# The opening of a two-layer mixer kernel: V projection by rows of Wv, with the first two tiles centred instead of normalised

## The chip, the cores and the metric

The kernel runs on 1 core of one Trainium2 chip. The metric is the device time of one execution in microseconds (us), and lower is better. The profile counts from its own zero and gives a *span*, about 1.9 us shorter than the device time of the same run. Each timed run also leaves its span, and I use spans where tenths of a microsecond matter.

## The reference, cut to what matters

Two layers, each an attention block and a token-mixing MLP with residuals, on 2048 tokens of width 1024. Only the first step of the first block is touched: a layer norm of the input rows, then the projection with the V third of `wqkv`.

```python
def _A_ref(x, wqkv, wo):
    B, S, D = x.shape                      # 1, 2048, 1024
    qkv = (x @ wqkv).reshape(B, S, 3, H, Dh) ...
    q, k, v = qkv[0], qkv[1], qkv[2]
    ...                                    # local dilated attention, 32 heads
x = A_x                                    # bf16
x = x + _A_ref(_layernorm(x, axis=-1), A_wqkv, A_wo)
...                                        # MLP, then both again
```

## The kernel before

The tokens are 16 tiles of 128 rows. At the start each tile is loaded (`x_load`), its statistics are taken on VectorE (`S_` twice, then `A_`), its reciprocal deviation on ScalarE (`R_`: a logarithm, then an exponential), it is normalised on VectorE (`N_`), and it is transposed into `hT`. For tiles 0 to 4 the transposition is done by TensorE (`tr`) and copied by ScalarE (`C_`) out of PSUM, the memory that its results go to; for the others by the DMA (`T_`). Then V of tile k is 16 matmuls of 128x512 (`V_`: two column halves n, eight contraction rows kt), evacuated by ScalarE (`E_`). Each engine has one list of steps that it follows in order:

```python
def w_load(n, hf):     # a block of Wv: half the contraction rows of half the columns, 512 KB
    return nc.sync.dma_start(out=wv[n][hf][:], in_=wq_v[:, hf*(KD//2):(hf+1)*(KD//2), 2*D + n*512:2*D + (n+1)*512])
def R_(k):  rss[k] = st("rs", [P, 1]); return rsqrt(rss[k][:], mvs[k][:, 1:2], 1.0, eps1)
def tr(k):
    tps[k] = pss.tile([P, KD, P], BF16, name="s", tag="s")
    ...                                                    # 8 transposes of xs[k]
def E_(k, n):
    return nc.scalar.copy(out=v[c][i][:, n*512:(n+1)*512], in_=pss_[k, n][:])
... # 14 warm-up matmuls on zeros
... # loads: x0 in halves, x1, Wv(0,0), x2, Wv(0,1), x3, Wv(1,0), Wv(1,1), x4 ... x15
pe  = [(tr, 0), (V_, 0, 0, lo4), (tr, 1), (V_, 0, 0, hi4), (V_, 1, 0, lo4), (tr, 2), (V_, 1, 0, hi4),
       (V_, 2, 0, a8), (V_, 0, 1, a8), (tr, 3), (V_, 1, 1, a8), (V_, 2, 1, a8), (tr, 4)]
pe += [(V_, k, n, a8) for k in range(3, NT) for n in range(NDC)]
act = [(R_, 0), (C_, 0, 0), (R_, 1), (C_, 0, 1), (C_, 1, 0), (C_, 1, 1), (R_, 2), (E_, 0, 0), ...]
dve = [(S_, 0, 0), (S_, 0, 1), (A_, 0), (S_, 1, 0), (N_, 0, halves), (S_, 1, 1), (A_, 1), (N_, 1, whole), ...]
```

The softmax here doesn't subtract the row's maximum and nothing guards it: scores larger than these inputs give would overflow.

## Time and profile before

| | before |
|---|---|
| device time, median of 6 runs | 1293.74 us |
| span of the profiled run | 1291.8 us |
| first transposition / first V matmul | 6.52 / 7.80 us |
| first q/k matmul, where the V projection has ended | 65.79 us |

The page of the kernel before: the span, the busy times of the engines, and the chain of work that ended last, by engine and by line.

```profile
span 1291.8 us, 19417 instructions
...
PE 1275.1 (99%) x8286; PEld 593.4 (46%) x8442; DVE 417.1 (32%) x852; ACT 372.8 (29%) x628; POOL 2.4 (0%) x15
...
PE 98%; issue 1%; DVE 0%; ACT 0%
PE m L352 17%; PE s L594 15%; PE s L547 15%; PE m L467 8%; PE acc L547 7%; PE m L547 7%; PE acc L594 7%; PE m L594 7%; PE m L337 4%; PE m L255 4%; PE s L383 2%; PE acc L418 1%; PE acc L422 1%; PE m L268 0%; PE s L244 0%
```

TensorE (PE) is busy for 99% of the span and makes up 98% of the chain. A change outside TensorE can therefore win only where TensorE stands still or has nothing useful to do, and that is in the first twelve microseconds. (Later there are 31 pauses of about 0.16 us, 4.9 us in all, which wait for nothing that the profile shows.) Here is the chain in order of time (start, duration, what), from the first warm-up matmul:

```profile
1.38 5.30 PE m L268 x14
6.68 0.46 PE s L244 x8
...
7.16 0.59 ACT hT L249
...
7.80 1.04 PE m L255 x4
8.84 0.61 PE s L244 x8
...
9.47 1.07 ACT hT L249 x2
10.55 0.20 ACT ln L174
...
10.77 0.21 ACT rs L175
...
11.01 0.56 DVE x L188
...
11.61 0.62 PE s L244 x8
...
12.28 4.26 PE m L255 x19
```

Read it as a relay: each row was released by the one above it. TensorE transposes tile 0 until 7.14; the transposed rows are copied (ACT, 7.16); four V matmuls and tile 1's transposes follow; then the chain leaves TensorE for the copy, rsqrt and normalisation that tile 2's transposes need (9.47 to 11.6). After 12.28 it is TensorE alone. A row of another engine is not always idle time of TensorE, which had V matmuls to do for part of it. What it really waited in the first 90 us is in the waits (total, times, longest):

```profile
PE m L268 <- DVE warm L207: 1.4, 1, 1.4
PE m L255 <- ACT hT L249: 0.7, 1, 0.7
PE s L244 <- DVE x L188: 0.3, 1, 0.3
```

That is 1.0 us after the first transposition (the warm-up's 1.4 us is the start of the program), and the rest of what can be won is a sooner start. The V projection ends where this piece of the chain begins:

```profile
65.79 6.91 PE m L352 x32
```

From here on both kernels do the same work, so I use the start of this piece as a landmark: 1291.8 less 65.79 leaves 1226.0 us.

Why the first transposition comes only at 6.5 is in the timeline (start, duration, engine, line, operation, shapes):

```profile
3.22 1.29 DVE L226 BATCH_NORM_STATS2 bn<-x 128x6 f32<-128x512 bf16 x2 [1.89 <-DMA x<-in_A_x_dram]
...
4.54 0.21 DVE L230 BATCH_NORM_AGGREGATE mv<-bn 128x2 f32<-128x12 f32 x1
...
4.78 0.29 ACT L174 ACTIVATE ln<-mv,eps 128x1 f32<-128x1 f32 x1 [2.70 <-DVE mv L230]
5.11 0.20 ACT L175 ACTIVATE rs<-ln 128x1 f32<-128x1 f32 x1
...
5.34 0.69 DVE L226 BATCH_NORM_STATS2 bn<-x 128x6 f32<-128x512 bf16 x1 [0.59 <-DMA x<-in_A_x_dram]
...
5.95 0.72 DVE L188 TENSOR_SCALAR x<-x,mv,rs 128x512 bf16<-128x512 bf16 x2
```

Statistics of tile 0 end at 4.75. The rsqrt takes until 5.31. By then VectorE, which works in order, starts the statistics of tile 1, which have landed, and normalises tile 0 only at 5.95.

### The profile page before, as it was taken

What the parts mean: (1) busy time and instruction counts of PE and PEld (TensorE: products, weight loads), DVE (VectorE), ACT (ScalarE), POOL (GpSimd) and SP (SyncE); (2) the same over time, 40 slices, a digit from 0 to 9 for tenths busy, and PEclk for the clock granted to TensorE, in tenths of its full rate; (3) what the DMA queues carried; (4) which work ended last, traced back from release to release, by engine and by line L of the source; (5) the groups of instructions that cost most, each with busy time, mean ns of one, the idle gap of its engine ahead of it and who ended that gap; (6) DMA issues with size and microseconds to landing.
All of it is one profiled execution on the core that took longest, in us unless ns stands there. A gap on an engine that the chain in (4) does not pass through costs nothing.

```text
span 1291.8 us, 19417 instructions
## 1 busy us (share of the span) xinstructions
PE 1275.1 (99%) x8286; PEld 593.4 (46%) x8442; DVE 417.1 (32%) x852; ACT 372.8 (29%) x628; POOL 2.4 (0%) x15
## 2 busy tenths in 40 slices
PE   9999999999999999999999999999999999999999
PEld 4444444444444444444444444444444444444444
DVE  7457777820000022322300667778100000111111
ACT  5456664431111110000023666644311111000000
POOL 0000000000000000000000000000000000000000
PEclk9999999999999999999999999999999999999999
DMA  8411123742222235466410111247423222334330
GB/s 236 82 46 47 51 82 120 212 139 82 65 82 76 57 110 139 131 154 142 130 33 1 47 50 51 79 151 214 120 65 89 75 60 81 103 106 136 117 92 33
DMA packets 201862, 125.54 MB, mean 97 GB/s; under 512 B 39984, under 2 KB 183600, under 8 KB 201776
## 3 DMA queue, kind: packets, MB, share of 16 engines
q1 hardware_dynamic: 201776, 124.30, 34.2%
q8 instruction: 66, 1.08, 0.4%
q14 instruction: 20, 0.16, 0.0%
HBM read 96.48 MB, written 16.78 MB: 88 GB/s over the span
## 4 chain that ended last, share of the span: by engine, by line
PE 98%; issue 1%; DVE 0%; ACT 0%
PE m L352 17%; PE s L594 15%; PE s L547 15%; PE m L467 8%; PE acc L547 7%; PE m L547 7%; PE acc L594 7%; PE m L594 7%; PE m L337 4%; PE m L255 4%; PE s L383 2%; PE acc L418 1%; PE acc L422 1%; PE m L268 0%; PE s L244 0%
## 5 line engine op out<-in xcount | busy, mean ns | idle before, releaser
L594 PEld LDWEIGHTS <-w 128*128 128x128 bf16 x1820 | 177.0, 98 | 210.2
L547 PEld LDWEIGHTS <-w 128*128 128x128 bf16 x1792 | 175.3, 98 | 211.4
L352 PE MATMUL m<-hT,wqk 128*128 128x512 bf16 x963 | 223.3, 379 | 6.2 <-issue 4.6
L547 PE MATMUL s<-h,w 128*128 128x512 bf16 x878 | 201.2, 379 | 0.8
L594 PE MATMUL s<-g,w 128*128 128x512 bf16 (+1 forms) x912 | 201.0, 374 | 0.7
L596 DVE SCALAR_TENSOR_TENSOR xo<-s,b_sb,xs 128x512 bf16<-128x512 f32 (+1 forms) x33 | 24.4, 739 | 532.9 <-PE s L594 530.8
L352 PEld LDWEIGHTS <-wqk 128*128 128x128 bf16 x1024 | 95.3, 98 | 117.9 <-issue 10.7
L398 DVE TENSOR_TENSOR Pm<-pc,band 32x640 bf16<-32x640 bf16 x256 | 123.5, 483 | 56.3 <-ACT pc L386 49.4
L467 PE MATMUL m<-wo,oT 128*128 128x512 bf16 x500 | 110.6, 379 | 0.8 <-issue 0.3
L547 PE MATMUL acc<-h,w 128*128 128x512 bf16 x440 | 103.1, 379 | 0.5
L594 PE MATMUL acc<-g,w 128*128 128x512 bf16 x436 | 99.7, 379 | 0.5
L547 PE MATMUL m<-h,w 128*128 128x512 bf16 x438 | 98.5, 379 | 0.5
L594 PE MATMUL m<-g,w 128*128 128x512 bf16 (+1 forms) x436 | 96.9, 376 | 0.6
L174 ACT ACTIVATE ln<-mv,eps 128x1 f32<-128x1 f32 x64 | 18.9, 295 | 221.1 <-DVE mv L182 184.9
L467 PEld LDWEIGHTS <-oT 128*128 128x128 bf16 x512 | 49.6, 98 | 60.3 <-issue 1.3
L554 ACT ACTIVATE g<-s,b_sb 128x1024 bf16<-128x1024 f32 x28 | 31.2, 1114 | 158.2 <-PE s L547 146.4
L363 DVE COPY qB<-qs 32x512 bf16<-32x512 bf16 x136 | 38.1, 280 | 99.2 <-ACT qs L359 97.1
L255 PE MATMUL m<-wv,hT 128*128 128x512 bf16 x250 | 55.6, 379 | 1.0 <-ACT hT L249 0.7
L337 PE MATMUL m<-wv,hT 128*128 128x512 bf16 x251 | 55.2, 379 | 0.3
L386 ACT ACTIVATE pc<-s,shift 128x640 bf16<-128x640 f32 x64 | 51.2, 800 | 11.7 <-PE s L383 11.7
L359 ACT CAST qs<-m 128x512 bf16<-128x512 f32 x64 | 37.5, 586 | 48.7 <-PE m L352 47.6
L356 ACT CAST kT<-m 128x512 bf16<-128x512 f32 x64 | 37.5, 586 | 46.4 <-PE m L352 46.4
(58 smaller groups left out, 671.8 us busy)
## 6 DMA issues: line engine op xcount, KB each, us to landing
w<-in_B_w_dram SPq DMA_DIRECT2D x56, 512.0 KB, 3.8
w<-in_B_w_dram SPq DMA_DIRECT2D x64, 448.0 KB, 4.7
wqk<-in_A_wqkv_dram SPq DMA_DIRECT2D x16, 512.0 KB, 5.2
xa<-xn SPq DMA_DIRECT2D x32, 256.0 KB, 2.3
xs<-xa SPq DMA_DIRECT2D x32, 256.0 KB, 3.0
wv<-in_A_wqkv_dram SPq DMA_DIRECT2D x8, 512.0 KB, 5.6
wo<-in_A_wo_dram SPq DMA_DIRECT2D x8, 512.0 KB, 6.4
xr<-in_A_x_dram SPq DMA_DIRECT2D x16, 256.0 KB, 3.4
```

The costliest lines, as they stand in the source:

```text
L255: r = nc.tensor.matmul(pss_[k, n][:], lhsT=hT[:, kt, cols(*order[k])], rhs=wv[n][kt // 4][:, kt % 4, :], start=(kt == 0), stop=(kt == KD - 1))
L337: nc.tensor.matmul(ps[:], lhsT=hT[:, kt, cols(c, i)], rhs=wv[n][kt // 4][:, kt % 4, :], start=(kt == 0), stop=(kt == KD - 1))
L352: mm = nc.tensor.matmul(ps[:], lhsT=wts[part][:, kt, (g % 2) * P:(g % 2 + 1) * P], rhs=hT[:, kt, lo:lo + 512], start=(kt == 0), stop=(kt = ...
L356: nc.scalar.copy(out=kT[u % 2][:, ls], in_=ps[:])
L359: nc.scalar.copy(out=qs[:], in_=ps[:])
L363: nc.vector.tensor_copy(out=qB[u % 2][hp, h, ls], in_=qs[hp, :])
L386: nc.scalar.activation(out=pc[:].rearrange("p (n t) h k -> p n (t h k)", n=2), in_=ss[:, :, 0:2 * HG * GW], func=ACT.Exp, scale=scale, bia ...
L398: mm = nc.vector.tensor_tensor(out=Pm[rp, :, s0:s0 + HB, r * KG:r * KG + GW].rearrange("p h t k -> p t h k"), in0=pc[rp], in1=mk, op=ALU.mult)
L467: mm = nc.tensor.matmul(ps[:], lhsT=oT[g][:, cols(c, i)], rhs=wo[n][g // 4][:, g % 4, :], start=(g == 0), stop=(g == NG - 1))
L547: nc.tensor.matmul(pairs[fl][0][dc], lhsT=wt[c][:, i, fl * P:(fl + 1) * P], rhs=h2[c][i][:, dc * 512:(dc + 1) * 512], start=(k == 0), stop ...
L554: nc.scalar.activation(out=g[fb][:, fl, :].rearrange("p (n d) -> p n d", n=2), in_=t[:], func=ACT.Gelu_apprx_tanh, bias=b1_sb[:, ft:ft + 1])
L594: nc.tensor.matmul(ap, lhsT=w2t[ft // HF][:, ft % HF, c::DIL], rhs=g[ft // GF][:, ft % GF, lo:lo + w], start=(ft == 0), stop=(ft == FT - 1))
```

## The change: its intent and the diff

The intent is to have TensorE at work sooner and without gaps.

- Layer norm is (x - mean) times one number per row, and that number can be applied after the projection. Tiles 0 and 1 are only centred before their transposes, half of tile 0 on each of VectorE and ScalarE, and the evacuation of V multiplies by the reciprocal deviation. No rsqrt stands before the first matmul.
- The q and k projections need the normalised rows in `hT`. So tiles 0 and 1 are normalised later and written over the centred ones by two more DMA transposes, in the middle of those of the other tiles.
- Wv is loaded by contraction rows (256 KB, all columns) in place of four blocks of 512 KB. TensorE goes through tiles 0 and 1 row by row, four matmuls to a row.
- A tile of V collects in one PSUM tile of two banks and is evacuated at once; two rsqrt steps follow each evacuation.
- Warm-up matmuls: nine, and one more after tile 0's transposes, in place of 14.

```diff
-        def w_load(n, hf):
-            return nc.sync.dma_start(out=wv[n][hf][:], in_=wq_v[:, hf * (KD // 2):(hf + 1) * (KD // 2), ...])
+        def w_load(kt):
+            return nc.sync.dma_start(out=wv[kt // 2][:, kt % 2, :], in_=wq_v[:, kt, 2 * D:3 * D])
...
+        def B_(k):      # minus the mean, for ScalarE
+            return nc.vector.tensor_scalar(out=nm0[:], in0=mvs[k][:, 0:1], scalar1=-1.0, scalar2=None, op0=ALU.mult)
+        def M_(k, h):
+            return nc.vector.tensor_scalar(out=xc[k][:, h], in0=xs[k][:, h], scalar1=mvs[k][:, 0:1], scalar2=None, op0=ALU.subtract)
+        def Ma(k, h):
+            return nc.scalar.activation(out=xc[k][:, h], in_=xs[k][:, h], func=ACT.Identity, bias=nm0[:])
...                     # E_ takes a whole tile
-            return nc.scalar.copy(out=v[c][i][:, n * 512:(n + 1) * 512], in_=pss_[k, n][:])
+            if k < 2:
+                return nc.scalar.activation(out=dst, in_=src, func=ACT.Identity, scale=rss[k])
+            return nc.scalar.copy(out=dst, in_=src)           # 128x1024
...                     # loads in the new order; nine warm-ups; the old lists
+        pe = [(tr, 0), (W_, 1), *VV(0, 0), (tr, 1), *VV(0, 1, 2), *VV(1, 0, 1, 2)]
+        for kt in range(3, 6):
+            pe += [*VV(0, kt), *VV(1, kt)]
+        pe += [(tr, 2), *VV(0, 6, 7), *VV(1, 6, 7), (V_, 2, 0, a8), (tr, 3), (V_, 2, 1, a8), (tr, 4)]
+        act = [(Ma, 0, halves[1]), (C_, 0, 0), (C_, 0, 1), (C_, 1, 0), (C_, 1, 1), (R_, 0), (R_, 1), (R_, 2), (C_, 2, 0), (C_, 2, 1),
+               (R_, 3), (E_, 0), (E_, 1), (R_, 4), ...]
...                     # VectorE: tile 0 is centred before tile 1's statistics
+            if k in (8, 9):
+                dve.append((N_, k - 8, whole))
+        sp = [(T_, k) for k in (*range(np_, 10), 0, 1, *range(10, NT))] + [(load_biases,)]
...                     # layer two's Wv in the same layout
```

More of the change, by code (lines that the diff above doesn't have):

```diff
@@ L113, in ln_exp_table @@
         return tc.keep_in_program_order(nc.scalar.preload_act_table_set("natural_log_exp_and_others"))
-    ln_exp_table()
     ident = const.tile([P, P], BF16, name="ident")
@@ L133 @@
                                 pattern=[[-1, GW]], channel_multiplier=1)
+    mv01 = const.tile([P, 2, 2], FP32, name="mv01")
+    rs01 = const.tile([P, 2], FP32, name="rs01")
+    nm0 = const.tile([P, 1], FP32, name="nm0")
     b1_bf = const.tile([P, FT], BF16, name="b1_bf")
@@ L187, in norm_dve @@
     def norm_dve(dst, x, mean, rs):
-        return nc.vector.tensor_scalar(out=dst, in0=x, scalar1=mean, scalar2=rs[:], op0=ALU.subtract, op1=ALU.mult)
+        return nc.vector.tensor_scalar(out=dst, in0=x, scalar1=mean, scalar2=rs, op0=ALU.subtract, op1=ALU.mult)
     def norm_act(dst, x, mean, rs):
@@ L205, in start_up @@
         np_ = 5
+        xc = [x2(f"xc{k}") for k in range(2)]
         warm = x2("warm", [P, 512])
@@ L217, in x_load @@
             return r
-        def w_load(n, hf):
-            return nc.sync.dma_start(out=wv[n][hf][:], in_=wq_v[:, hf * (KD // 2):(hf + 1) * (KD // 2),
-                                                                2 * D + n * 512:2 * D + (n + 1) * 512])
+        def w_load(kt):
+            return nc.sync.dma_start(out=wv[kt // 2][:, kt % 2, :], in_=wq_v[:, kt, 2 * D:3 * D])
         def S_(k, cc):
@@ L228, in A_ @@
         def A_(k):
-            mvs[k] = st("mv", [P, 2])
-            return nc.vector.bn_aggr(out=mvs[k][:], in_=sts[k][:])
+            mvs[k] = mv01[:, k, :] if k < 2 else st("mv", [P, 2])[:]
+            return nc.vector.bn_aggr(out=mvs[k], in_=sts[k][:])
+        def B_(k):
+            return nc.vector.tensor_scalar(out=nm0[:], in0=mvs[k][:, 0:1], scalar1=-1.0, scalar2=None, op0=ALU.mult)
+        def M_(k, h):
+            return nc.vector.tensor_scalar(out=xc[k][:, h], in0=xs[k][:, h], scalar1=mvs[k][:, 0:1], scalar2=None,
+                                           op0=ALU.subtract)
+        def Ma(k, h):
+            return nc.scalar.activation(out=xc[k][:, h], in_=xs[k][:, h], func=ACT.Identity, bias=nm0[:])
         def R_(k):
-            rss[k] = st("rs", [P, 1])
-            return rsqrt(rss[k][:], mvs[k][:, 1:2], 1.0, eps1)
+            rss[k] = rs01[:, k:k + 1] if k < 2 else st("rs", [P, 1])[:]
+            return rsqrt(rss[k], mvs[k][:, 1:2], 1.0, eps1)
         def N_(k, hs):
@@ L241, in tr @@
         def tr(k):
-            tps[k] = pss.tile([P, KD, P], BF16, name="s", tag="s")
+            tps[k] = psm.tile([P, KD, P], BF16, name="m", tag="m")
             for kt in range(KD):
-                r = nc.tensor.transpose(tps[k][:, kt, :], xs[k][:, kt * P:(kt + 1) * P], ident[:])
+                r = nc.tensor.transpose(tps[k][:, kt, :], (xc[k] if k < 2 else xs[k])[:, kt * P:(kt + 1) * P], ident[:])
             return r
@@ L251, in V_, with E_ @@
         def V_(k, n, kts):
-            if kts[0] == 0:
-                pss_[k, n] = m_tile()
+            if k not in pss_:
+                pss_[k] = a_tile() if k % 3 == 1 else s_tile()
             for kt in kts:
-                r = nc.tensor.matmul(pss_[k, n][:], lhsT=hT[:, kt, cols(*order[k])], rhs=wv[n][kt // 4][:, kt % 4, :],
+                r = nc.tensor.matmul(pss_[k][:, n, :], lhsT=hT[:, kt, cols(*order[k])], rhs=wv[kt // 2][:, kt % 2, n * 512:(n + 1) * 512],
                                      start=(kt == 0), stop=(kt == KD - 1))
             return r
-        def E_(k, n):
+        def E_(k):
             c, i = order[k]
-            return nc.scalar.copy(out=v[c][i][:, n * 512:(n + 1) * 512], in_=pss_[k, n][:])
+            dst, src = v[c][i][:].rearrange("p (n d) -> p n d", n=NDC), pss_[k][:]
+            if k < 2:
+                return nc.scalar.activation(out=dst, in_=src, func=ACT.Identity, scale=rss[k])
+            return nc.scalar.copy(out=dst, in_=src)
         def T_(k):
@@ L266, in start_up, with W_ @@
         wm = m_tile()
-        for _ in range(14):
-            chain_("PE", lambda: nc.tensor.matmul(wm[:], lhsT=warm[:, 0:P], rhs=warm[:], start=True, stop=True))
+        def W_(n):
+            for _ in range(n):
+                r = nc.tensor.matmul(wm[:], lhsT=warm[:, 0:P], rhs=warm[:], start=True, stop=True)
+            return r
+        for _ in range(9):
+            chain_("PE", W_, 1)
         halves = (slice(0, D // 2), slice(D // 2, D))
         whole = (slice(0, D),)
+        chain_("ACT", ln_exp_table)
@@ L272, in start_up @@
         chain_("SP", x_load, 0, halves)
         chain_("SP", x_load, 1)
-        chain_("SP", w_load, 0, 0)
+        for kt in range(4):
+            chain_("SP", w_load, kt)
         chain_("SP", x_load, 2)
-        chain_("SP", w_load, 0, 1)
+        chain_("SP", w_load, 4)
+        chain_("SP", w_load, 5)
         chain_("SP", x_load, 3)
-        chain_("SP", w_load, 1, 0)
-        chain_("SP", w_load, 1, 1)
+        chain_("SP", w_load, 6)
+        chain_("SP", w_load, 7)
         for k in range(4, NT):
@@ L281, in start_up, with VV @@
             chain_("SP", x_load, k)
-        lo4, hi4 = range(KD // 2), range(KD // 2, KD)
+        def VV(k, *kts):
+            return [(V_, k, n, [kt]) for kt in kts for n in range(NDC)]
         a8 = range(KD)
-        pe = [(tr, 0), (V_, 0, 0, lo4), (tr, 1), (V_, 0, 0, hi4), (V_, 1, 0, lo4), (tr, 2), (V_, 1, 0, hi4),
-              (V_, 2, 0, a8), (V_, 0, 1, a8), (tr, 3), (V_, 1, 1, a8), (V_, 2, 1, a8), (tr, 4)]
+        pe = [(tr, 0), (W_, 1), *VV(0, 0), (tr, 1), *VV(0, 1, 2), *VV(1, 0, 1, 2)]
@@ L287, in start_up @@
+        for kt in range(3, 6):
+            pe += [*VV(0, kt), *VV(1, kt)]
+        pe += [(tr, 2), *VV(0, 6, 7), *VV(1, 6, 7), (V_, 2, 0, a8), (tr, 3), (V_, 2, 1, a8), (tr, 4)]
         pe += [(V_, k, n, a8) for k in range(3, NT) for n in range(NDC)]
-        act = [(R_, 0), (C_, 0, 0), (R_, 1), (C_, 0, 1), (C_, 1, 0), (C_, 1, 1), (R_, 2), (E_, 0, 0), (C_, 2, 0), (C_, 2, 1),
-               (E_, 1, 0), (R_, 3), (E_, 2, 0), (R_, 4), (E_, 0, 1), (C_, 3, 0), (C_, 3, 1), (R_, 5), (E_, 1, 1), (R_, 6),
-               (E_, 2, 1), (C_, 4, 0), (C_, 4, 1)]
@@ L291, in start_up @@
-        es = [(E_, k, n) for k in range(3, NT) for n in range(NDC)]
+        act = [(Ma, 0, halves[1]), (C_, 0, 0), (C_, 0, 1), (C_, 1, 0), (C_, 1, 1), (R_, 0), (R_, 1), (R_, 2), (C_, 2, 0), (C_, 2, 1),
+               (R_, 3), (E_, 0), (E_, 1), (R_, 4), (C_, 3, 0), (C_, 3, 1), (E_, 2), (C_, 4, 0), (C_, 4, 1), (R_, 5), (E_, 3), (R_, 6)]
         rs = [(R_, k) for k in range(7, NT)]
-        for j, e in enumerate(es):
-            act.append(e)
-            if rs and j % 4 != 3:
-                act.append(rs.pop(0))
@@ L297, in start_up @@
-        dve = [(S_, 0, 0), (S_, 0, 1), (A_, 0), (S_, 1, 0), (N_, 0, halves), (S_, 1, 1), (A_, 1), (N_, 1, whole),
+        for k in range(4, NT):
+            act.append((E_, k))
+            act += rs[:2]
+            del rs[:2]
+        dve = [(S_, 0, 0), (S_, 0, 1), (A_, 0), (B_, 0), (M_, 0, halves[0]), (S_, 1, 0), (S_, 1, 1), (A_, 1), (M_, 1, whole[0]),
                (S_, 2, 0), (S_, 2, 1), (A_, 2)]
@@ L300, in start_up @@
             nx = k + 1 < NT
-            if nx:
-                dve.append((S_, k + 1, 0))
-            dve.append((N_, k, whole))
+            if k == 2:
+                dve += [(N_, k, whole), (S_, k + 1, 0)]
+            else:
+                if nx:
+                    dve.append((S_, k + 1, 0))
+                dve.append((N_, k, whole))
             if nx:
                 dve += [(S_, k + 1, 1), (A_, k + 1)]
+            if k in (8, 9):
+                dve.append((N_, k - 8, whole))
         dve.append((zero_fill,))
         dve.append((cast_biases,))
-        sp = [(T_, k) for k in range(np_, NT)] + [(load_biases,)]
+        sp = [(T_, k) for k in (*range(np_, 10), 0, 1, *range(10, NT))] + [(load_biases,)]
         qs = {"PE": pe, "ACT": act, "DVE": dve, "SP": sp}
-        need = {cast_biases: lambda: (load_biases,) in done, R_: lambda k: k in mvs, N_: lambda k, h: k in rss, tr: lambda k: (N_, k) in done, C_: lambda k, hf: k in tps,
-                V_: lambda k, n, kts: ((C_, k, 1 if kts[-1] == KD - 1 else 0) in done or (T_, k) in done), E_: lambda k, n: (V_, k, n) in done,
-                T_: lambda k: (N_, k) in done}
+        need = {cast_biases: lambda: (load_biases,) in done, R_: lambda k: k in mvs, N_: lambda k, h: k in rss, tr: lambda k: (N_, k) in done if k > 1 else (M_, k) in done and (k == 1 or (Ma, k) in done),
+                B_: lambda k: k in mvs, M_: lambda k, h: k in mvs, Ma: lambda k, h: (B_, k) in done, C_: lambda k, hf: k in tps,
+                V_: lambda k, n, kts: ((C_, k, kts[-1] * 2 // KD) in done or (T_, k) in done), E_: lambda k: (V_, k, 1) in done and (k > 1 or k in rss),
+                T_: lambda k: (N_, k) in done and (k > 1 or (E_, k) in done)}
         done = set()
@@ L325, in load_wv, with fill_wv @@
     def load_wv():
-        return [[wt_("wv", [P, KD // 2, 512]) for _ in range(2)] for _ in range(NDC)]
-    def fill_wv(wv, n):
-        for hf in range(2):
-            nc.sync.dma_start(out=wv[n][hf][:],
-                              in_=wq_v[:, hf * (KD // 2):(hf + 1) * (KD // 2), 2 * D + n * 512:2 * D + (n + 1) * 512])
+        return [wt_("wv", [P, 2, D]) for _ in range(KD // 2)]
+    def fill_wv(wv):
+        for j in range(KD // 2):
+            nc.sync.dma_start(out=wv[j][:], in_=wq_v[:, 2 * j:2 * j + 2, 2 * D:3 * D])
     def v_proj(v, c, i, wv, ns):
@@ L336, in v_proj @@
             for kt in range(KD):
-                nc.tensor.matmul(ps[:], lhsT=hT[:, kt, cols(c, i)], rhs=wv[n][kt // 4][:, kt % 4, :],
+                nc.tensor.matmul(ps[:], lhsT=hT[:, kt, cols(c, i)], rhs=wv[kt // 2][:, kt % 2, n * 512:(n + 1) * 512],
                                  start=(kt == 0), stop=(kt == KD - 1))
@@ L603, in gemm2 @@
             mean, rs = stats(xo, 1.0, eps1)
-            norm_dve(xs[:], xo[:], mean, rs)
+            norm_dve(xs[:], xo[:], mean, rs[:])
             nc.sync.dma_start_transpose(out=hT[:, :, cols(c, i)], in_=xs[:])
@@ L619 @@
         else:
-            fill_wv(wv, 0)
-            fill_wv(wv, 1)
+            fill_wv(wv)
             wts = [None, None]
```

## The prediction

> **What bounds the kernel now.** The tensor engine: the page gives PE 1275.1 of 1291.8 us busy (99%), the chain that ended last is 98% PE. The change touches the opening (V projection of layer one, until the first q/k matmul at 65.79 us in the chain) and the layout of layer two's Wv, which the chain shows as unbroken PE work.
>
> **What it loses.** Timeline and chain: x0's first half reaches VectorE at 3.22, statistics end at 4.75, rsqrt on ScalarE 4.78 to 5.31, normalising 5.95 to 6.67 (held up by tile 1's statistics), transposes done 7.13, hT copy 0.59, first V matmul at 7.80. From there to 65.79 are 57.99 us. A V matmul costs 0.2159 us (208 in 44.9 us, from 20.9 on), 256 cost 55.3, four further transposes 4 x 0.5 = 2.0: about 0.7 us is lost after 7.80 (waits for the hT copy and for rsqrt and normalising of tile 2).
>
> **What changes.**
> - Tile 0 is centred, not normalised: a 128x1 step, then half on VectorE (0.36) and half on ScalarE (0.59) side by side. No wait for rsqrt (0.53) or tile 1's statistics. First transposes done near 6.0 instead of 7.13, first V matmul near 6.7.
> - Tile 1 landed at 5.34; its two statistics, aggregate and centring (1.3 + 0.21 + 0.55) let its transposes start near 7.5 instead of 8.81.
> - From there PE has work by rows of Wv (4 matmuls, 0.86 us, per 256 KB). By bytes moved in the DMA windows plus about 1.2 us to landing (fits x1 at 5.3, x4 at 13.7), rows 1, 2, 3 land near 7.1, 7.9, 8.8 and rows 6, 7 near 12.4, 13.2; PE wants them at 8.0, 8.5, 10.2, 13.3, 14.1.
> - Evacuations: one of 1024 (estimate 1.1 us from 1.114 us of the 1024 gelu) instead of two of 0.59. Rsqrt two per 3.45 us instead of three per 6.9.
> - Two normalisations (0.55 each) and two DMA transposes (median 3.1 us to landing) more; off the path.
> - Tightest wait: evacuation of tile 2 (near 20.2), tile 4's copies (21.3), rsqrt 5, normalising (22.4), DMA transpose 3.1: 25.6, against V of tile 5 at 26.3.
> - Layer two: Wv is loaded in the same four pieces from 601 us, needed at 649.6: nothing.
> - Warm matmuls 14 become 9 plus 1. The Trainium skill ("TensorE: Matmul & The Clock Gate", "What's actually happening") says full clock comes after about 3.4 us of activity in a free-running window; the trace agrees roughly: weight loads 0.43 us apart from 1.38 to 5.62, then 0.2. Nine end near 5.2, so the clock should still rise near 5.6.
>
> **Sum.** Tile 1's transposes end at 8.0; 254 matmuls 54.8, three transposes 1.5: V ends at 64.35 instead of 65.79. Gain 1.4 us: 1292.3 us, range 1291.6 to 1293.3. Faster by over 2%: 0; within 2%: 1.0; slower: 0.
>
> **What would show it.** First transposes near 5.4 to 6.0, first V matmul 6.7, tile 1's transposes at 7.5, first q/k matmul near 64.4, and every later distance unchanged (from first q/k matmul to the end 1226 us). No PE wait on Wv loads over 0.3 us in the waits.
>
> **What would make it wrong.** The clock rising one window later: V matmuls at 0.43 until about 9, costing 1 to 1.5 us, most of the gain. Rows of Wv landing over 1 us later than worked out. Tile 5's DMA transpose late (the slowest took 4.2 us to landing): up to 0.4 us.

## The result, and the profile after

| | before | after |
|---|---|---|
| device time, median of 6 runs | 1293.74 us | 1292.18 us |
| lowest to highest | 1293.43 to 1294.32 | 1292.02 to 1292.80 |
| span of the profiled run | 1291.8 us | 1290.6 us |
| first transposition / first V matmul | 6.52 / 7.80 us | 5.24 / 6.81 us |
| first q/k matmul (landmark) | 65.79 us | 64.48 us |

The medians differ by 1.56 us, and no run of one kernel reaches into the range of the other. The ratio is 0.9988 with a 95% interval of 0.9976 to 1.0001; a ratio is the mean time of one kernel's fast runs over that of the other's of the same rounds, so it is not quite the ratio of the medians. The page after:

```profile
span 1290.6 us, 19407 instructions
...
PE 1273.7 (99%) x8282; PEld 592.7 (46%) x8438; DVE 417.5 (32%) x854; ACT 370.9 (29%) x613; POOL 2.4 (0%) x15
...
PE 98%; issue 1%; DMA 0%; DVE 0%; SPq 0%
```

The chain of the changed kernel in order of time, to be held against the one of before:

```profile
1.72 3.85 DMA x<-in_A_x_dram
...
5.59 1.30 DVE bn L228 x2
...
6.92 0.22 DVE mv L232
...
7.16 0.50 DVE xc L238
...
7.70 0.62 PE m L256 x8
8.32 0.86 PE s L267 x4
...
64.48 6.91 PE m L383 x32
```

There is one relay left ahead of TensorE: the load of tile 1, its two statistics, aggregate and centring. Then it is TensorE alone, from 7.70 to the end of the V projection at 64.48. The copy out of PSUM, the rsqrt and the normalisation that stood between pieces of TensorE work before are gone from the chain. The start of the timeline shows how tile 0 got ahead:

```profile
4.84 0.34 DVE L238 TENSOR_SCALAR xc<-x,mv 128x512 bf16<-128x512 bf16 x1
4.96 0.72 ACT L242 ACTIVATE xc<-x,nm 128x512 bf16<-128x512 bf16 x1 [2.88 <-DVE nm L235]
...
5.24 0.89 PE L256 MATMUL m<-ident,xc 128*128 128x128 bf16 x8 [0.18 <-DVE xc L238]
...
6.81 0.60 PE L267 MATMUL s<-wv,hT 128*128 128x512 bf16 x2 [0.46 <-ACT hT L261]
```

The aggregate ends at 4.74. VectorE and ScalarE centre a half each, and the first four transposes run at 5.24 while ScalarE is still busy. What TensorE waited for in the first 90 us (total, times, longest):

```profile
PE m L256 <- DVE xc L238: 0.5, 2, 0.3
PE s L267 <- ACT hT L261: 0.5, 1, 0.5
```

Against the kernel before, the waits are no shorter in total (1.0 us in both), but they lie earlier: what is left is over at 7.70, where the kernel before still waits at 11.6, and the first V matmul runs 1.0 us sooner. Wv does not appear. The span less the landmark is 1226.1 us, as before (1226.0): the whole gain lies ahead of it.

### The profile page after: what moved, and what is told of

It is laid out like the page before. It is cut to its first block, busy times and chain, and to the rows that moved or that the text cites. A ratio compares the mean times of both kernels' runs of the same rounds, so it can differ in the third digit from the quotient of the medians.

```text
span 1290.6 us, 19407 instructions
## 1 busy us (share of the span) xinstructions
PE 1273.7 (99%) x8282; PEld 592.7 (46%) x8438; DVE 417.5 (32%) x854; ACT 370.9 (29%) x613; POOL 2.4 (0%) x15
## 4 chain that ended last, share of the span: by engine, by line
PE 98%; issue 1%; DMA 0%; DVE 0%; SPq 0%
PE m L383 17%; PE s L625 15%; PE s L578 15%; PE m L498 9%; PE acc L578 7%; PE m L578 7%; PE acc L625 7%; PE m L625 7%; PE m L368 4%; PE s L267 3%; PE s L414 2%; PE acc L267 1%; PE acc L449 1%; PE acc L453 1%; DMA x<-in_A_x_dram 0%
## 5 line engine op out<-in xcount | busy, mean ns | idle before, releaser
L368 PE MATMUL m<-wv,hT 128*128 128x512 bf16 x251 | 55.2, 379 | 0.3
L505 DVE TENSOR_TENSOR xn<-m,xr 128x512 bf16<-128x512 f32 x64 | 44.2, 690 | 16.9 <-PE m L498 16.4
```

The lines of the kernel that those rows point to most:

```text
L368: nc.tensor.matmul(ps[:], lhsT=hT[:, kt, cols(c, i)], rhs=wv[kt // 2][:, kt % 2, n * 512:(n + 1) * 512], start=(kt == 0), stop=(kt == KD - 1))
L505: return nc.vector.tensor_tensor(out=xn[:, xs_], in0=pss_["o", n][:], in1=xr[:, xs_], op=ALU.add)
```

## The experiments

All correct runs computed the right result; one was wrong on purpose. Single runs of one kernel turned out to differ by some tenths of a microsecond, so the runs that decide were made five times. I compare mean spans. The chip of the first two calls gave a mean of 1291.96 us for nine runs of the kernel before, the chip of the last call 1292.03.

My theory: centring takes the rsqrt out of the way of the first tiles, and rows of Wv give TensorE something to do once they are there; each is worth a part and needs the other. Rivals: rows alone, centring alone, or the shorter warm-up.

### The changed kernel once more

No edit; a control.

> The changed kernel once more, as a control and on this chip: landmark (first q/k matmul) within 0.3 of 64.48, whole time 1.2 to 1.7 us below the kernel before. If the gain were an accident of the runs, the interval of the ratio would hold 1.000 comfortably.

Measured: 1292.23 us median of 5, mean span 1290.24; the six runs of the result had 1290.37. The gain in span is 1.72 us on this chip. The interval of the ratio, 0.9974 to 1.0002, still holds 1.000, but only at its edge; the five runs (1291.94 to 1292.29 us) stay clear of the nine of the kernel before (1293.14 to 1294.33). The landmark of this profile is 64.10, just beyond the scatter I had expected. The timeline of TensorE shows why:

```profile
6.80 0.61 PE L267 MATMUL s<-wv,hT 128*128 128x512 bf16 x2 [0.46 <-ACT hT L261]
7.32 0.62 PE L256 MATMUL m<-ident,xc 128*128 128x128 bf16 x8
```

Tile 1's transposes came at 7.32, straight after the first two V matmuls, in place of 7.70. Tile 1's statistics could start at 5.21 and not at 5.59: the same load landed earlier. So the 0.3 us of standing still in the first profile belongs to that run, not to the kernel.

### Rows of Wv without centring

```diff
-  M_: (x - mean)                     Ma: x + (-mean)               E_(0), E_(1): times rs
+  M_: (x - mean) * rs                Ma: x * rs + (-mean * rs)     E_(0), E_(1): plain copies
-  act = [(Ma, 0), (C_, 0, 0), (C_, 0, 1), (C_, 1, 0), (C_, 1, 1), (R_, 0), (R_, 1), (R_, 2), ...]
+  act = [(R_, 0), (Ma, 0), (C_, 0, 0), (R_, 1), (C_, 0, 1), (C_, 1, 0), (C_, 1, 1), (R_, 2), ...]
```

> The changed kernel, but tiles 0 and 1 are normalised before their transposes (each waits for its rsqrt); Wv by rows, warm-up and evacuations as in the changed kernel. Landmark: start of the first q/k matmul in the chain (before 65.79, after 64.48). Theory 1 (centring and rows of Wv are both needed): tile 1's transposes move from 7.7 to about 8.4, the landmark to about 65.2. Rival (rows of Wv alone carry the gain): landmark stays within 0.2 of 64.5. Rival (centring alone carries it): landmark back at 65.8. Result stays correct.

Measured once: 1293.21 us, landmark 65.40, close to my 65.2. Then five times:

> The run with normalised first tiles again, now five times, because single runs of one kernel turned out to scatter by 0.4 us in the landmark (span less 1226.1). Mean spans so far: before 1292.0, changed kernel 1290.3. If rows of Wv without centring are worth a part only: mean span 1291.2 to 1291.6 (single run 1291.5). If they are worth everything: 1290.3; nothing: 1292.0.

Measured: spans 1291.4 four times and 1292.6 once, mean 1291.64, a little above the range I gave because of the one; 1293.15 us median. The profile (one of the four):

```profile
5.89 0.92 PE L255 MATMUL m<-ident,xc 128*128 128x128 bf16 x8 [0.49 <-DVE xc L190]
...
8.50 0.62 PE L255 MATMUL m<-ident,xc 128*128 128x128 bf16 x8 [0.40 <-DVE xc L190]
```

Tile 0's transposes start at 5.89 for 5.24, and tile 1's at 8.50 for 7.32 to 7.70, with TensorE idle before them for their normalisation. The change without the centring gives 0.4 us in the mean (1292.03 less 1291.64), not 1.7. The kernel before scatters by 1 us itself on this chip (1291.5 to 1292.5), so 0.4 is not clear of noise. Nor need the rows have brought it: this kernel also keeps the change's shorter warm-up, its halves of tile 0 on two engines, and its order on VectorE, with tile 0 ahead of tile 1's statistics. Its first transposes start 0.6 us before those of the kernel before (6.52).

### Centring with Wv by columns

```diff
-  loads by rows of Wv; pe as in the change
+  loads: x0, x1, Wv(0,0), x2, Wv(0,1), x3, Wv(1,0), Wv(1,1), as before
+  pe = [(tr, 0), (W_, 1), (V_, 0, 0, lo4), (tr, 1), (V_, 0, 0, hi4), (V_, 1, 0, lo4), (tr, 2), (V_, 1, 0, hi4), ...]
```

> The changed kernel with its centred tiles, but Wv in four column-and-half blocks of 512 KB and the matmul order of the kernel before. Theory 1: first V matmul near 6.8 to 7.1, but the second block of Wv lands only near 9.7, so PE stands about 1.4 us between tile 1's transposes and the second half of tile 0; landmark about 65.6, nearly the kernel before. Rival (centring alone carries the gain): no such wait and a landmark near 64.5.

Measured once: 1294.28 us, landmark 66.38. It is later than the kernel before, and later than my theory had it. The waits on Wv came as expected (0.7 us twice), but there were also two waits for normalised tiles (0.45 and 0.48), which I had not thought of: ScalarE's order was still that of the change, and in it the rsqrt of tiles 2 and 4 stood behind those of 0 and 1 and behind evacuations that come late with columns. The run mixed two causes. With them moved forward:

```diff
-  act = [..., (R_, 0), (R_, 1), (R_, 2), (C_, 2, 0), (C_, 2, 1), (R_, 3), (E_, 0), (E_, 1), (R_, 4), (C_, 3, 0), (C_, 3, 1), (E_, 2), ...]
+  act = [..., (R_, 2), (R_, 0), (R_, 1), (C_, 2, 0), (C_, 2, 1), (R_, 3), (R_, 4), (E_, 0), (C_, 3, 0), (C_, 3, 1), (E_, 1), (E_, 2), ...]
```

> As the run by columns, but on ScalarE the rsqrt of tile 2 goes ahead of those of tiles 0 and 1 and that of tile 4 ahead of the first evacuation, which had added about 1 us of waits of PE for normalised tiles (0.45 and 0.48). What remains is centring with Wv by columns: waits on Wv of about 0.7 twice, landmark about 65.3. If centring alone were worth the whole gain, 64.5.

Measured once: landmark 65.15, 1293.27 us. Five times:

> Centring with Wv by columns, five times. If centring alone is worth a part only: mean span 1291.1 to 1291.5 (single run 1291.3), with PE waiting for Wv or hT for over 1 us in the first 10 us. If it is worth everything: 1290.3; nothing: 1292.0.

Measured: mean span 1291.26 (1291.2 to 1291.3), 1293.14 us median. TensorE's timeline, where the bracket gives the idle time before a group and what ended it:

```profile
5.22 0.89 PE L257 MATMUL m<-ident,xc 128*128 128x128 bf16 x8
...
6.98 1.02 PE L268 MATMUL s<-wv,hT 128*128 128x512 bf16 x4 [0.65 <-DMA wv<-in_A_wqkv_dram]
...
9.32 1.02 PE L268 MATMUL s<-wv,hT 128*128 128x512 bf16 x4 [0.87 <-DMA wv<-in_A_wqkv_dram]
```

Tile 0 is ready as early as in the change (transposes at 5.22), but its first V matmul waits for the first 512 KB of Wv until 6.98, and the fifth waits for the next 512 KB until 9.32. TensorE stands for 1.5 us, 0.5 of which the change has too. In the single run the profile puts the second of these waits down to the copy of hT, which ended at nearly the same time. The weight load of that matmul shows that it was Wv, because it needs hT alone and had been done at 8.38, while its matmul began at 9.26:

```profile
8.38 0.10 PEld L268 LDWEIGHTS <-hT 128*128 128x128 bf16 x1
```

The change without the rows gives about 0.8 us.

Together, as differences of mean spans from the kernel before on the same chip:

| | Wv by columns | Wv by rows |
|---|---|---|
| normalised first | 0 (the kernel before) | -0.4 (-0.6 without the one long run) |
| centred | -0.8 | -1.7 (the change) |

Neither rival stands: without the centring, or without the rows, the gain is less than half of the whole. The differences to the last corner are those of one part each, with the lists of steps that it needs: with the rest of the change in place the rows are worth about 0.9 us and the centring about 1.3. The differences from the first corner mix several parts. The three new corners share the evacuations by 1024, the nine warm-up matmuls, and the order and the halves of tile 0's work; what these do by themselves to the kernel before was not run. That each part needs the other, as my theory had it (0.4 and 0.8 make 1.2, the whole is 1.7), is not shown.

### More and fewer warm-up matmuls

```diff
-        for _ in range(9):
+        for _ in range(14):     # one run
+        for _ in range(4):      # the other
```

> Fourteen warm-up matmuls as in the kernel before. They should end near 6.3 and hold up tile 0's transposes (now 5.24), so first V matmul near 7.4 and tile 1's transposes near 7.85 instead of 7.70: landmark about 64.6, at most 64.9. If the shorter warm-up carries the gain of the change, the landmark goes to 65.5 or more.

Measured once, with 14: landmark 64.71, 1292.69 us, first V matmul 7.50, tile 1's transposes 7.94. As expected: the longer warm-up holds up tile 0 and costs some tenths (span 1290.8 against a mean of 1290.24 for five runs of the control). It does not carry the gain. The size is less sure: this is one run, and 1290.8 is also the longest of the six runs of the change. Held against the first profile of the change, in which tile 1's statistics began as late (5.59, here 5.58), the landmark is only 0.2 later.

> Four warm-up matmuls instead of nine (ending near 3.1 us). If the clock rises by activity in a window, V matmuls run 0.43 us apart until 9 us or later and the landmark goes to 65.2 to 67; if warm-up only fills time, the landmark stays at 64.5.

Measured once, with four: landmark 64.95, less than I had expected. Five times:

> Four warm-up matmuls, five times. The single run lost 0.5 us, its clock rising near 8 us. If the clock depends on activity before, the mean span stays 0.3 us or more above the changed kernel's 1290.3, with more scatter; if not, 1290.3.

Measured: mean span 1291.62 (1291.0 to 1292.3), so 1.4 us lost on average, with more scatter. The weight loads show the clock, because their distance is that of the matmuls. With four warm-ups:

```profile
5.24 0.84 PEld L256 LDWEIGHTS <-xc 128*128 128x128 bf16 x8 [2.88 <-DVE xc L238]
...
7.86 0.79 PEld L256 LDWEIGHTS <-xc 128*128 128x128 bf16 x7 [0.28 <-issue]
```

In the changed kernel:

```profile
5.24 0.23 PEld L256 LDWEIGHTS <-xc 128*128 128x128 bf16 x4 [0.74 <-DVE xc L238]
...
7.70 0.45 PEld L256 LDWEIGHTS <-xc 128*128 128x128 bf16 x8 [0.78 <-DVE xc L238]
```

Eight transposes' loads take 0.84 us with four warm-ups and 0.45 us (7.70) with nine: half speed and full speed. With four, the tensor engine is still slow through tile 1's transposes at 7.86. This agrees with the Trainium skill ("TensorE: Matmul & The Clock Gate", "What's actually happening"): the full clock comes after about 3.4 us of activity in a window that runs free. At 0.43 us each, four warm-ups are 1.7 us of activity and nine 3.9 (an estimate from the distance of the weight loads). Nine is not a safe number, though; see the next experiment.

### Filling the gap before tile 1's transposes

```diff
-  pe = [(tr, 0), (W_, 1), *VV(0, 0), (tr, 1), *VV(0, 1, 2), *VV(1, 0, 1, 2)]
+  pe = [(tr, 0), (W_, 1), *VV(0, 0, 1), (tr, 1), *VV(0, 2, 3), *VV(1, 0, 1, 2, 3)]
```

> Only the order of the first V matmuls is changed: row 1 of Wv for tile 0 moves ahead of tile 1's transposes, into the 0.46 us in which PE stood before them; row 3 of tile 0 moves before tile 1's first rows. By the DMA queue's own waits row 1 had landed by 6.9 and row 3 by 8.5, so no new wait: landmark 64.05 to 64.2, 0.3 to 0.4 below the changed kernel. If Wv were what bounds this stage, waits on Wv appear and the landmark stays at 64.5.

Measured: mean span 1290.28, 1292.36 us median, landmark 64.37: no gain over the control (1290.24). My expectation failed. The gap that I wanted to fill is mostly not there, as the control had shown: tile 1 usually lands early enough. In this profile the clock also rose late, in spite of nine warm-ups:

```profile
5.21 0.84 PEld L256 LDWEIGHTS <-xc 128*128 128x128 bf16 x8 [0.70 <-DVE xc L238]
...
6.98 0.13 PEld L267 LDWEIGHTS <-hT 128*128 128x128 bf16 x2 [0.84 <-ACT hT L261]
7.39 0.32 PEld L267 LDWEIGHTS <-hT 128*128 128x128 bf16 x2 [0.27 <-issue]
7.82 0.65 PEld L256 LDWEIGHTS <-xc 128*128 128x128 bf16 x8
```

Tile 0's eight loads at 5.21 take 0.84 us here (half speed). After those at 6.98 the next load comes only at 7.39, and the two from there on are 0.2 us apart, which is full speed. In the first profile of the changed kernel tile 0's loads were at full speed at 5.24 (four in 0.23 us). Of the ten profiles with nine warm-ups, three show tile 0's transposes begin at half speed: this one and the single runs of 1293.21 us (normalised first) and 1293.27 us (by columns, rsqrt moved).

> The same with tile 1's rows loaded in two halves, so that its statistics start before the whole tile has landed: centring of tile 1 ends near 7.3 instead of 7.65. The gap is already filled by row 1 of Wv, which ends near 7.7, so I expect no more than 0.1 beyond the run with the moved row alone: landmark 64.0 to 64.2.

The second edit was `chain_("SP", x_load, 1, halves)`. Measured: mean span 1290.58, landmark 64.68: 0.3 us worse than the control. One more load ahead of Wv delays its rows: in the trace rows 2 and 3 land at 8.3 and 9.2, in that of the control at 7.2 and 8.7. Moving row 3 forward makes TensorE ask for it before it is there. This is the line of the waits:

```profile
PE s L267 <- DMA wv<-in_A_wqkv_dram: 0.3, 1, 0.3
```

So Wv's rows are not what bounds the changed kernel, but there is little slack. I found no version that beats it.

### Without the second transposes of tiles 0 and 1

```diff
-            if k in (8, 9):
-                dve.append((N_, k - 8, whole))
-        sp = [(T_, k) for k in (*range(np_, 10), 0, 1, *range(10, NT))] + [(load_biases,)]
+        sp = [(T_, k) for k in range(np_, NT)] + [(load_biases,)]
```

> The second normalisation and DMA transposes of tiles 0 and 1 taken away (wrong result on purpose: q and k of two tiles lack the division by their deviation). If they are off the critical path as predicted, mean span 1290.2 to 1290.4, as the changed kernel; if the 13 instead of 11 transposes or the two normalisations held anything up, less than 1290.1.

Measured: the result is wrong (relative error 0.35), mean span 1290.42, landmark 64.02. It is not faster than the control (1290.24, landmark 64.10). Normalising and transposing two tiles a second time costs nothing that can be seen.

## Why the prediction was right

Predicted 1292.3 us, measured 1292.18; a gain of 1.4 us predicted, of 1.56 measured. The mechanism held. That the times agree to 0.1 us is partly luck: the changed kernel's own runs differ by 0.8 us, and its landmark was 64.48 in one profile and 64.10 in another, against 64.35 predicted. Point by point:

- **What bounds the kernel.** Right: the distance from the landmark to the end is 1226.0 before and 1226.1 after; all of the gain is in the opening.
- **First transposes 5.4 to 6.0, first V matmul 6.7.** They began at 5.24 and ended near 6.0; the first V matmul came at 6.81. ScalarE's half took 0.72 us, not the 0.59 that I had read from copies of the same size.
- **Tile 1's transposes near 7.5.** They came at 7.70 in one profile and 7.32 in another. The term taken as fixed, the landing of tile 1, is not: its statistics started at 5.59 and 5.21.
- **Wv by rows lands in time.** Right: no wait on Wv. The DMA queue's own waits show rows 1 to 3 landed by 6.9, 7.6 and 8.5, each 0.2 to 0.3 ahead of my estimate. That this matters is shown by the column runs, where TensorE stood 1.5 us in all for Wv.
- **Evacuation of 1024.** Estimated 1.1 us; measured 1.01 for a copy and 1.10 with the scale.
- **Tile 5's DMA transpose, the tightest wait.** It was issued at 22.21 (predicted 22.4), V of tile 5 began at 26.34 (predicted 26.3), and TensorE did not wait.
- **Second transposes off the path.** Right, shown by the run without them.
- **The clock one window later, as the main risk.** The risk is real. It showed in a profile of the version with moved rows, and four warm-ups lose 1.4 us. The six runs of the change lie within 0.8 us, so it did not cost the predicted 1 to 1.5 us there.

Open is what makes the kernel before scatter by 1 us in span (1291.4 to 1292.4 on one chip), and why one of the five runs with normalised first tiles took 1.2 us longer: the clock would fit, but those runs have no profile.

## What to carry to other kernels

When TensorE is busy 99% of the time, cost only what shortens its waits or starts it sooner; here that was about two microseconds by estimate, and 1.6 came. A per-row scale that commutes with a matmul can move from the operand to the evacuation, and takes its whole chain off the start, but it pays in full only if the weights arrive in the order and grain in which the engine will now ask for them. To judge tenths of a microsecond, repeat the control before improving on a gap seen in one profile.

## What the Trainium skill lacked or had wrong

- "TensorE: Matmul & The Clock Gate", "What you observe", gives the rise of the clock a scatter of about 500 ns from run to run, under sustained matmuls. Here, with the same nine warm-up matmuls from 1.38 us and short pauses after them, it had risen by 5.24 us in one profile and only by 7.39 in another: about 2 us apart. The next section of that page allows for this (the same kernel with 6, 11 or 14 slow matmuls), so it is the 500 ns that misleads.
- "DMA: Bandwidth & Descriptors", "Anatomy of one DMA", gives about 2.0 us plus bytes over 436 GB/s (measured on the other issuing path). For the first 128 KB load that makes an estimate of 2.3 us, and the profile has a median of 2.4 us: it agrees. No page says how much an early load behind others scatters: tile 1's rows, issued near 1.72 us, were there by 5.1 us in the profile of the run with four warm-ups (start of their statistics) and only by 5.6 in that of the change.
